# Weight conversion from 64-bit words: the sign set by a scaling of negative upper words on ScalarE instead of by a step of its own on VectorE

## The chip, the cores and the metric

The kernel runs on one core of a Trainium2 chip. The metric is the time of one execution on the device, in microseconds (us). The engines are named as the profile names them: PE is TensorE's matmul and PEld its weight load, DVE is VectorE, ACT is ScalarE, POOL is GpSimd, and SP is the queue that issues the DMAs. Each engine runs its own list of instructions strictly in order and waits on semaphores of the others.

## The reference, cut to what matters

The five weight matrices w_k, w_r, w_v, w_in and w_out come as float64, the other inputs as float32.

```python
scores = q @ k.T / sqrt(64); scores += minimum(-(cum_i - cum_j), 0), causal   # 4 x 8 heads, 576 rows
x = softmax(scores) @ v                                                       # 4 x 576 x 512
xk, xr = mix(x, x_prev, mu_k), mix(x, x_prev, mu_r)
y = sigmoid(xr @ w_r) * (relu(xk @ w_k) ** 2 @ w_v)
h = gelu(y @ w_in); u, v = halves of h
out = y + (u * (w_sg @ layernorm(v) * g + b)) @ w_out
```

## The kernel before, in words

The weights come to the chip as pairs of 32-bit words, and the kernel makes float32 values of them itself. A weight matrix is cut into parts of 128 rows by 512 columns: 8 of w_k (wk00 to wk31), 4 of w_r, 8 of w_v, 8 of w_in and 4 of w_out, 32 in all. `load_words` (L102) loads the words of one part, 512 KB, into a tile such as `wk00w`. `assemble` makes the float32 part in a buffer `cvt`: ACT scales the upper word, read as a float32 number, by 2^-112 (L111), which leaves room in the exponent; DVE shifts the bits left by 3 (L114), puts the sign bit of the upper word back (L115), and puts in the top 3 bits of the lower word (L116). `convert` then splits the part into a rounded half (ACT, L71 or L124) and the rest (DVE, L74 or L125), which the matmuls take.

The first 20 parts are converted while the first eight attention jobs run (a job is one pair of heads; the first four jobs are the first 320 rows of the first batch, the next four its other 256 rows, and from the ninth on a job has all rows of its batch). Two buffers `cvt` take turns. A load of words runs five parts ahead, and it is held back by a copy of one column (L101, DVE) from the `cvt` that was finished last into the tile that is to be loaded. The tiles of w_v lie where a table for the gate of the scores, `gt`, lay before; so the first of these copies, `wv00w`, also has to wait until the two DMAs that take that table away (`gate_d<-gt`, L320) have landed.

A job's scores go from PE (L362) through DVE (L377, mask and row minimum, in a bank of PSUM) to ACT (L404, exponential), PE (L442, transposes), ACT (L444, copies), PE (L446 and L450, products with v), DVE (L472, L473, L475) and back by PE and ACT (L478, L479) to the tile `xt`. When the first four jobs have their part of `xt`, the mixing (L617, L623, L71, L74) and the large matmuls (L685) can start. All engines work through lists that a scheduler of the builder has written out beforehand; a loop over priorities decides which work is near which. All DMAs are issued from SP's one list, each on one of eight semaphores in turn, and each waits for the transfer eight places ahead of it.

Of the kernel before, what the change touches and what calls it, by code (L numbers as in the profile page):

```python
# [8 lines left out]
F32 = mybir.dt.float32  # L9
# [4 lines left out]
AF = mybir.ActivationFunctionType  # L14
ALU = mybir.AluOpType
# [37 lines left out]
def block_kernel(ctx: ExitStack, tc: tile.TileContext, qkv, vb, s, w_r, w_k, w_v, mu, w_in, w_out, w_sgT, g_ln, b_sg, out):  # L53
# [6 lines left out]
    nc = tc.nc  # L60
# [44 lines left out]
    def assemble(w, c, n, t):  # L105

        pool, name, raw = w.parts[c][n]
        words = raw.bitcast(I32).rearrange("p (n t) -> p n t", t=2)
        hw, lw = words[:, :, 1], words[:, :, 0]
        ti = t.bitcast(I32)  # L110
        i = nc.scalar.mul(t, hw.bitcast(F32), 2.0**-112)  # L111
        if 0 < len(exps) <= GC:
            behind(i, exps[-1])
        nc.vector.tensor_scalar(ti, ti, 3, None, ALU.logical_shift_left)  # L114
        nc.vector.scalar_tensor_tensor(ti, hw, -0x80000000, ti, ALU.bitwise_and, ALU.bitwise_or)  # L115
        nc.vector.scalar_tensor_tensor(ti, lw, 29, ti, ALU.logical_shift_right, ALU.bitwise_or)  # L116
        return pool, name

    def convert(w, c, n, t):

        pool, name = assemble(w, c, n, t)
        half = pool.tile([P, 2, 512], F32R, tag=name, name=name)
        if w is wv:
            nc.scalar.mul(half[:, 0], t, 0.5)  # L124
            nc.vector.scalar_tensor_tensor(half[:, 1], t, 0.5, half[:, 0].bitcast(F32), ALU.mult, ALU.subtract)  # L125
        else:
            copy("A" if att is not None else "D", half[:, 0], t)
            minus(ENG["cl"], half[:, 1], t, half[:, 0])
        w.parts[c][n] = half
# [31 lines left out]
    def behind(i, j):  # L161

        kind = mybir.DependencyInfo(mybir.DependencyClass.NoSync, mybir.DependencyReason.DATA)
        tc.add_manual_dep(i.ins, j.ins.name, kind)
# [909 lines left out]
    def quarters(last):  # L1074

        ta = w1p.tile([P, 2, 512], F32, tag="wk01", name="cvt")
        tb = w1p.tile([P, 2, 512], F32, tag="wr30", name="cvt")
        for c in range(4):
            load_words(wo, c, 0)
        for c in range(4):  # L1080
            assemble(wo, c, 0, (ta, tb)[c // 2][:, c % 2])
        a11, a21, a12, a22 = (t[:, :, i * 256 : (i + 1) * 256] for t in (ta, tb) for i in range(2))

        def split(name, pool, tag, x):
            w = wq[name] = pool.tile([P, 2, 2, 256], F32R, tag=tag, name="w" + name)
            behind(nc.scalar.copy(w[:, 0], x), last[5 if name[0] == "s" else 3])
            minus("D", w[:, 1], x, w[:, 0])

        def fold(dst, x, y, op):
            nc.vector.tensor_tensor(dst, x, y, op)  # L1090

        split("11", w1p, "wk00", a11)
        split("12", w1p, "wk10", a12)
        split("22", w1p, "wk20", a22)
        fold(a22, a21, a22, ALU.add)
        split("s1", w1p, "wk30", a22)
        fold(a21, a11, a21, ALU.subtract)
        fold(a11, a22, a11, ALU.subtract)
        split("s3", xtp, "xh", a21)
        fold(a12, a12, a11, ALU.subtract)  # L1100
        split("s4", xtp, "xl", a12)
        split("s2", w1p, "wr30", a11)
# [93 lines left out]
```

## Time and profile before

| what | us |
| --- | --- |
| three timed runs | 679.87, 681.18 (median), 681.36 |
| the profiled execution, its time | 680.43 |
| its span, first to last instruction | 678.6 |
| busy: PE, DVE, ACT, POOL | 658.1, 543.2, 427.9, 48.3 |

The span is 1.8 us shorter than the profiled execution's own time, which lies 0.75 us below the median of the timed runs. PE is busy for 97% of the span, but the profile takes a waiting time inside a row of matmuls as busy, so the shares have to be read stage by stage.

### The profile page before, as it was taken

The page shows a single profiled execution, that of the slowest core. Times are in us where ns is not written, and L with a number is a line of the kernel's source. Part 1 is how long each engine was busy: PE and PEld are TensorE (multiplying, and loading weights), DVE is VectorE, ACT ScalarE, POOL GpSimd, SP SyncE. Part 2 cuts the span into 40 slices and gives each one's busy share as a digit, 9 for nine tenths or more (in the row PEclk, how much of TensorE's full clock was granted, in tenths as well). Part 3 has the DMA queues.
Part 4 walks back from the last instruction along what each step waited for, and adds up shares of the span by engine and source line. Part 5 has one row for each costly group of instructions (what it writes and reads, how often), then busy time and mean ns, then how long its engine had stood idle before and what let it go on. Part 6 is the DMA issues. An engine that isn't in the chain of part 4 may idle for free.

```text
span 678.6 us, 12902 instructions
## 1 busy us (share of the span) xinstructions
PE 658.1 (97%) x4590; PEld 613.2 (90%) x4590; DVE 543.2 (80%) x1396; ACT 427.9 (63%) x1014; POOL 48.3 (7%) x95
## 2 busy tenths in 40 slices
PE   7899999999999999999999999999999999999997
PEld 4667979798888989998999999999998998998997
DVE  8999988988889998898886696731788786958857
ACT  5788887779869987996895655714554423234222
POOL 6110000001110111011100000000000000000003
PEclk8899999999999999999999999999999999999999
DMA  8897132353343334333200840004131150340302
GB/s 269 265 300 233 40 105 73 106 156 98 106 132 94 110 96 115 119 95 101 86 24 19 297 134 35 1 18 159 54 122 36 44 167 1 112 135 0 97 1 71
DMA packets 41400, 71.66 MB, mean 106 GB/s; under 512 B 8244, under 2 KB 23968, under 8 KB 41304
## 3 DMA queue, kind: packets, MB, share of 16 engines
q1 hardware_dynamic: 41336, 70.84, 33.5%
q8 instruction: 36, 0.59, 0.4%
q14 instruction: 28, 0.23, 0.1%
HBM read 56.29 MB, written 10.19 MB: 98 GB/s over the span
## 4 chain that ended last, share of the span: by engine, by line
PE 73%; DVE 11%; DMA 5%; ACT 5%; issue 3%; SPq 1%; POOL 1%; POOLq 0%; DVEq 0%; ACTq 0%
PE m L685 28%; PE pu L698 8%; PE ps L995 3%; PE av L534 3%; PE t L549 3%; PE pg L959 3%; PE pg L960 2%; PE pg L958 2%; PE pv L890 2%; PE pv L889 2%; PE pv L888 2%; PE p L995 2%; PE av L450 2%; DVE ptl L553 2%; PE s L362 2%
## 5 line engine op out<-in xcount | busy, mean ns | idle before, releaser
L404 ACT ACTIVATE pr<-pr,nm 128x448 f32<-128x448 f32 (+4 forms) x144 | 84.8, 591 | 13.6 <-DVE nm L377 13.1
L685 PE MATMUL m<-xh,wk 128*128 128x288 f32 x512 | 87.4, 302 | 0.4 <-ACT kf L645 0.3
L685 PE MATMUL m<-kh,wv 128*128 128x288 f32 x512 | 79.3, 296 | 0.0
L685 PEld LDWEIGHTS m<-xh,wk 128*128 128x128 f32 x512 | 73.5, 189 | 2.8 <-ACT kf L645 1.0
L685 PEld LDWEIGHTS m<-kh,wv 128*128 128x128 f32 x512 | 71.9, 188 | 0.8
L377 DVE CUSTOM_DVE_ANT_0 pr<-s,mask 128x320 f32<-128x320 f32 (+3 forms) x128 | 60.4, 476 | 8.4 <-PE s L365 6.1
L74 DVE TENSOR_TENSOR xl<-xf,xh 128x288 fp32r<-128x288 f32 (+1 forms) x80 | 40.4, 519 | 18.5 <-ACT xh L824 12.7
L552 ACT CAST pth<-t 128x512 fp32r<-128x512 f32 (+1 forms) x72 | 38.0, 532 | 13.0 <-PE t L549 12.0
L645 ACT ACTIVATE kf<-m 128x288 f32<-128x288 f32 x64 | 26.1, 408 | 31.6 <-PE m L685 31.2
L685 PE MATMUL m<-xl,wk 128*128 128x288 f32 x256 | 45.9, 298 | 0.0
L553 DVE TENSOR_TENSOR ptl<-t,pth 128x512 fp32r<-128x512 f32 (+1 forms) x72 | 43.9, 615 | 2.4 <-ACT pth L552 2.0
L74 DVE TENSOR_TENSOR kl<-kf,kh 128x576 fp32r<-128x576 f32 x32 | 24.8, 775 | 23.8 <-ACT kh L71 23.7
L685 PE MATMUL m<-kl,wv 128*128 128x288 f32 x256 | 43.2, 298 | 0.0
L364 PE MATMUL s<-qk 128*128 128x288 f32 (+4 forms) x132 | 41.1, 313 | 1.0 <-DVE nh L377 0.4
L549 PE MATMUL t<-early,pr 128*128 128x128 f32 x252 | 39.0, 274 | 2.7 <-DVE ptl L553 2.6
L685 PE MATMUL m<-xh,wr 128*128 128x288 f32 x256 | 41.0, 299 | 0.4 <-ACT kf L645 0.3
L365 PE MATMUL s<-qk 68*128 68x288 f32 (+4 forms) x132 | 39.9, 308 | 0.4 <-DMA qk<-gate_d 0.4
L698 PE MATMUL pu<-xh,wi 128*128 128x288 f32 x256 | 40.2, 295 | 0.0
L617 ACT ACTIVATE xf<-xt,mu 128x288 f32<-128x288 f32 x64 | 33.6, 536 | 8.2 <-DVE xl L74 4.6
L685 PEld LDWEIGHTS m<-xl,wk 128*128 128x128 f32 x256 | 37.9, 188 | 0.7 <-issue 0.4
L959 PE MATMUL pg<-wg,vh 128*128 128x288 f32 x128 | 37.8, 295 | 0.0
L960 PE MATMUL pg<-wg,vl 128*128 128x288 f32 x128 | 37.7, 295 | 0.0
(330 smaller groups left out, 1757.3 us busy)
## 6 DMA issues: line engine op xcount, KB each, us to landing
qld<-qkv SPq DMA_DIRECT2D x24, 288.0 KB
kld<-qkv SPq DMA_DIRECT2D x24, 288.0 KB
x_d<-rt SPq DMA_DIRECT2D x8, 576.0 KB
xf<-x_d SPq DMA_DIRECT2D x8, 576.0 KB
vld<-qkv SPq DMA_DIRECT2D x24, 160.0 KB
qk<-qk SPq DMA_DIRECT2D x24, 144.0 KB
ot<-x_d SPq DMA_DIRECT2D x24, 144.0 KB
outT<-ot SPq DMA_DIRECT2D x24, 144.0 KB
```

Of the source, the lines that this page charges most:

```text
L74: (nc.gpsimd if pick(engines) == "P" else nc.vector).tensor_tensor(dst, a, b.bitcast(F32), ALU.subtract)
L364: nc.tensor.matmul(dst, qk[0][:, 0, qs], qk[0][:, 1, ks], start=True, stop=False)
L365: issued[0] = nc.tensor.matmul(dst, qk[1][0 : D + 4, 0, qs], qk[1][0 : D + 4, 1, ks], start=False, stop=True)
L377: nc.vector.tensor_tensor_reduce(out=dst, in0=src, in1=msk, scale=-0.125, scalar=first, op0=ALU.add, op1=ALU.min, accum_out=acc)
L404: i = nc.scalar.activation(dst, dst, AF.Exp, bias=nm[:, col : col + 1], scale=-1.0, accum_out=acc)
L549: issued[0] = nc.tensor.transpose(bank[:, o : o + P], x, ident)
L552: nc.scalar.copy(pth[:, cols], bank[:, 0:o])
L553: nc.vector.tensor_tensor(ptl[:, cols], bank[:, 0:o], pth[:, cols].bitcast(F32), ALU.subtract)
L685: i = nc.tensor.matmul(dst, w(x, c, m), xx[:, c], start=(n + c == 0), stop=(n == 2 and c == w.nk - 1))
L698: nc.tensor.matmul(dst, w(x, c, m), xx[:, c], start=(n + c == 0), stop=(n == 2 and c == w.nk - 1))
L959: nc.tensor.matmul(pg[:, 0:HD], vh[k][:, ds], wg[1][k][:, hs], start=False, stop=False)
L960: nc.tensor.matmul(pg[:, 0:HD], vl[k][:, ds], wg[0][k][:, hs], start=False, stop=False)
```

## The change

ACT's scaling becomes a Prelu with the same scale: positive values are only scaled, negative ones are multiplied by a further -2^32. Their result is positive and has one more bit set in its exponent field, and the shift left by 3 moves this bit into the place of the sign. The instruction that put the sign in is dropped.

```diff
         ti = t.bitcast(I32)
-        i = nc.scalar.mul(t, hw.bitcast(F32), 2.0**-112)
+        i = nc.scalar.activation(t, hw.bitcast(F32), AF.Prelu, scale=2.0**-112, alpha=-(2.0**32))
         if 0 < len(exps) <= GC:
             behind(i, exps[-1])
         nc.vector.tensor_scalar(ti, ti, 3, None, ALU.logical_shift_left)
-        nc.vector.scalar_tensor_tensor(ti, hw, -0x80000000, ti, ALU.bitwise_and, ALU.bitwise_or)
         nc.vector.scalar_tensor_tensor(ti, lw, 29, ti, ALU.logical_shift_right, ALU.bitwise_or)
         return pool, name
```

From the dropped line on, the lines of the changed kernel have a number that is one lower: its L115 is the former L116, L376 the former L377, L319 the former L320, and so on.

The scheduler writes the lists anew, and they differ in two stretches: from the first conversion to the start of the second batch's attention, and around the parts of w_in and w_out. Between these two stretches DVE's and ACT's lists are the same, instruction for instruction.

SP's list before, from the load of part wk31 to the load of `vb` for the fourth job. `gate_d<-gt` are the two DMAs for which the column copy `wv00w` waits, `kld`, `vld` and `qld` are inputs of the second batch:

```order
L102 DMA wk31w<-w_k 128x512
L213 DMA kld<-qkv 128x576
L223 DMA vld<-qkv 128x320
L102 DMA wr00w<-w_r 128x512
L213 DMA qld<-qkv 128x576
L213 DMA kld<-qkv 128x576
L223 DMA vld<-qkv 128x320
L320 DMA gate_d<-gt 16x4608 x2
L219 DMA vb<-vb 128x390
```

The same place in the list of the changed kernel:

```order
L102 DMA wk31w<-w_k 128x512
L102 DMA wr00w<-w_r 128x512
L212 DMA kld<-qkv 128x576
L222 DMA vld<-qkv 128x320
L212 DMA qld<-qkv 128x576
L212 DMA kld<-qkv 128x576
L222 DMA vld<-qkv 128x320
L319 DMA gate_d<-gt 16x4608
L102 DMA wr20w<-w_r 128x512
L319 DMA gate_d<-gt 16x4608
L218 DMA vb<-vb 128x390
```

The load of wr00w has moved ahead of four inputs, and that of wr20w, which stood eight places behind the second `gate_d`, now stands ahead of it. The second `gate_d` has the place eight behind the load of wr00w, where before it had the place eight behind wk31w.

DVE's list before, around the column copy `wv00w`. `pr` and `nm` are the scores of a job and their row minimum:

```order
L377 ISA pr_88,nm<-s,mask 128x192
L377 ISA nm 128x1
L114 TENSOR_SCALAR cvt<-cvt 128x512
L377 ISA pr_434,nm<-s,early 128x128
L377 ISA nm 128x1
L116 SCALAR_TENSOR_TENSOR cvt<-wk21w,cvt 128x512
L115 SCALAR_TENSOR_TENSOR cvt<-wk11w,cvt 128x512
L101 COPY wv00w<-cvt 128x1
L472 TENSOR_SCALAR rc<-av 128x4
L116 SCALAR_TENSOR_TENSOR cvt<-wk11w,cvt 128x512
```

The same place in the list of the changed kernel:

```order
L114 TENSOR_SCALAR cvt<-cvt 128x512
L115 SCALAR_TENSOR_TENSOR cvt<-wk11w,cvt 128x512
L376 ISA pr_89,nm<-s,mask 128x320
L376 ISA nm 128x1
L376 ISA pr_88,nm<-s,mask 128x192
L376 ISA nm 128x1
L101 COPY wr30w<-cvt 128x1
L101 COPY wv00w<-cvt 128x1
L74 TENSOR_TENSOR wk_405<-cvt,wk_405 128x512
L471 TENSOR_SCALAR rc<-av 128x4
```

The copy has kept its place against the scores of the third job, apart from the 128x128 block, which now comes after it; the conversion of wk11 is finished ahead of the copy instead of behind it.

SP's list before, a little later: from the load of wr20w to the inputs of the fifth job (`qk_86<-qkv`, `vb`):

```order
L102 DMA wr20w<-w_r 128x512
L102 DMA wr10w<-w_r 128x512
L204 DMA qk_86<-qkv 64x2x576
L207 DMA qk_86<-cur_d 1x576
L208 DMA qk_86<-cur_d 1x576
L102 DMA wv00w<-w_v 128x512
L204 DMA qk_86<-qkv 64x2x576
L219 DMA vb<-vb 128x650
```

The same place in the list of the changed kernel:

```order
L102 DMA wr10w<-w_r 128x512
L102 DMA wr30w<-w_r 128x512
L102 DMA wv00w<-w_v 128x512
L218 DMA vb<-vb 128x650
L203 DMA qk_86<-qkv 64x2x576
L206 DMA qk_86<-cur_d 1x576
L207 DMA qk_86<-cur_d 1x576
L203 DMA qk_86<-qkv 64x2x576
```

The fifth job's first input now stands behind three loads of words and its `vb`; before, it stood behind two loads of words.

## Rows read from the trace of the kernel before

**Rows 1.** The page's first two parts: busy time, and slices of 17 us.

```profile
PE 658.1 (97%) x4590; PEld 613.2 (90%) x4590; DVE 543.2 (80%) x1396; ACT 427.9 (63%) x1014; POOL 48.3 (7%) x95
DVE  8999988988889998898886696731788786958857
DMA  8897132353343334333200840004131150340302
```

**Rows 2.** Windows: stretch, its length, busy us (instructions) by engine, clock, DMA share, GB/s.

```profile
10.00:34.00 24.00, 20.64 (x109) 14.29 (x108) 21.63 (x68) 19.01 (x43) 3.69 (x7) 0.87 0.91 291
34.00:60.00 26.00, 24.49 (x148) 17.41 (x146) 25.42 (x84) 22.69 (x52) 2.23 (x3) 1.00 0.94 281
60.00:100.00 40.00, 38.74 (x274) 34.66 (x274) 37.15 (x97) 35.43 (x73) 0.00 (x0) 1.00 0.29 90
100.00:360.00 260.00, 253.11 (x1838) 239.36 (x1837) 228.83 (x607) 215.87 (x556) 25.75 (x42) 1.00 0.34 101
360.00:400.00 40.00, 39.70 (x294) 38.75 (x293) 27.54 (x58) 22.86 (x49) 1.60 (x2) 1.00 0.52 175
400.00:640.00 240.00, 240.00 (x1658) 231.02 (x1657) 169.66 (x416) 99.43 (x213) 0.00 (x0) 1.00 0.22 70
```

**Rows 3.** Windows of line L115 alone: DVE busy us (instructions).

```profile
0.00:34.00 34.00, 4.79 (x7) 0.90 0.85 267
34.00:100.00 66.00, 8.91 (x13) 1.00 0.54 165
370.00:400.00 30.00, 4.17 (x6) 1.00 0.66 223
400.00:490.00 90.00, 4.07 (x6) 1.00 0.17 57
```

**Rows 4.** Timeline of DVE: start, us, what, idle time before it.

```profile
31.61 0.28 DVE L377 CUSTOM_DVE_ANT_0 pr<-s,early 128x128 f32<-128x128 f32 x1
31.82 0.08 DVE L377 DVE_READ_ACCUMULATOR2_ANT nm<- 128x1 f32 x1
...
32.42 0.68 DVE L115 SCALAR_TENSOR_TENSOR cvt<-wk11w,cvt 128x512 int32<-128x512 int32 x1
34.04 0.15 DVE L101 COPY wv00w<-cvt 128x1 f32<-128x1 f32 x1 [0.94 <-DMA vb<-vb]
34.14 0.16 DVE L472 TENSOR_SCALAR rc<-av 128x4 f32<-128x4 f32 x1
34.22 0.68 DVE L116 SCALAR_TENSOR_TENSOR cvt<-wk11w,cvt 128x512 int32<-128x512 int32 x1
34.82 0.69 DVE L74 TENSOR_TENSOR wk<-cvt,wk 128x512 fp32r<-128x512 f32 x1
...
52.86 0.42 DVE L475 TENSOR_TENSOR avt<-av,rc 128x256 f32<-128x256 f32 x1
53.71 0.43 DVE L114 TENSOR_SCALAR cvt<-cvt 128x512 int32<-128x512 int32 x1 [0.43 <-ACT cvt L111]
54.05 0.68 DVE L115 SCALAR_TENSOR_TENSOR cvt<-wv00w,cvt 128x512 int32<-128x512 int32 x1
54.66 0.62 DVE L377 CUSTOM_DVE_ANT_0 pr<-s,mask 128x448 f32<-128x448 f32 x1
55.20 0.08 DVE L377 DVE_READ_ACCUMULATOR2_ANT nm<- 128x1 f32 x1
```

**Rows 5.** Timeline of SP's queue: when it issues which DMA.

```profile
20.65 0.38 SPq L102 DMA_DIRECT2D wk31w<-w_k  x1
...
24.21 1.88 SPq L320 DMA_DIRECT2D gate_d<-gt  x2
26.55 0.35 SPq L219 DMA_DIRECT2D vb<-vb  x1
```

**Rows 6.** The chain that ended last up to 110 us: by line, and one piece.

```profile
by line: PE m L685 14.6%; PE av L450 13.2%; PE s L362 11.5%; DMA vb<-vb 6.8%; DMA qld<-qkv 5.9%; PE t L442 3.8%; PE av L446 3.2%; DVE cvt L115 3.0%; issue 2.9%; DVE cvt L116 2.4%; DVE pr L377 2.3%; SPq L204 2.3%; DMA qk<-gate_d 2.0%; DVE wk
...
26.55 7.50 DMA vb<-vb
```

**Rows 7.** ACT by line: a table load, an exponential group, a scaling.

```profile
L264 ACT ACT_TABLE_LOAD  x1: 1283/1283/1283, 0.7 to 0.7; - x1
L404 ACT ACTIVATE pr<-pr,nm 128x576 f32<-128x576 f32 x8 | 6.2, 779 | 1.0 <-DVE nm L377 0.8
L111 ACT ACTIVATE cvt<-wk00w x1: 652/652/652, 11.5 to 11.5; 128x512 f32<-128x512 f32 x1
```

## What I predict, and why

> **What bounds the kernel now.** I read the page first. PE is busy for 97% of the span, and DVE's slices are fullest in the left half [rows 1]: the kernel has stages, and each has its own bound. The windows by stage say which. From 400 to 640 us PE is busy for all 240.00 us, so nothing that DVE or ACT gains there counts. From 100 to 360 us PE lacks 6.89 us, spread over attention work that the change doesn't touch. From 10 to 60 us it lacks 3.36 + 1.51 = 4.87 us, from 60 to 100 us 1.26 us, from 360 to 400 us 0.30 us [rows 2]. That is all that a faster conversion can find on PE: 4.87 + 1.26 + 0.30 = 6.4 us, plus what is hidden in matmuls that the profile lengthens while they wait.
>
> In the stretch from 10 to 60 us three things are nearly full: DVE with 21.63 of 24 and 25.42 of 26 us, the DMA engines with shares of 0.91 and 0.94, and ACT with 19.01 and 22.69 us [rows 2]. The page alone suggests DVE. But the one long idle time of DVE in it, 0.94 us, ends at 34.04 with a transfer [rows 4], and the chain of work holds a transfer of 7.50 us that ends at the same moment [rows 6]. So I ask of every microsecond that DVE saves whether a transfer lets it through.
>
> **What is removed.** L115 goes 32 times: 7 before 34 us, 13 from there to 100 us, 6 around w_in, 6 after 400 us [rows 3]. One lasts 0.68 us and holds the next instruction back by 0.60 (34.22 to 34.82 for its like, 54.05 to 54.66 for itself) [rows 4]. That frees 7 x 0.60 = 4.2 us of DVE before 34 us and 13 x 0.60 = 7.8 us up to 100 us. The 6 after 400 us lie under a PE that never waits: nothing. Those around w_in can give at most the 0.30 us that PE lacks there; I take 0.2.
>
> **What ACT pays.** The trace has no Prelu. Below, it costs what the scaling costs, 0.652 us; above, it costs what an ACT instruction with a per-row operand costs, 0.779 us for 576 columns [rows 7], scaled by 512/576 to 0.69 us, some 0.04 more, 0.8 us for 20 parts. It reads the same words and has constant operands like the scaling, so I take nothing.
>
> **What the first 4.2 us become.** DVE must pass the column copy wv00w, which waits for the two gate_d transfers. They were issued from 24.21 us on and let DVE go at 34.04 [rows 4, 5]. The name beside the wait, vb, is a transfer of SP's next row that DVE doesn't read; the table's own transfers stand directly ahead of it. DVE would reach the copy up to 3.8 us earlier than before (7 instructions less, 4.2 us; the end of wk11's conversion ahead of it, 0.6 us more; a 128x128 block behind it, 0.2 less). But the transfers don't come earlier: the loads ahead of them keep the DMA engines at a share of 0.91. They come later, for a load of 512 KB has moved ahead of the second one. At the 291 GB/s of this stretch [rows 2] its 524,288 bytes take 1.80 us; the lower bound is nothing, if it fills the 9% that is free; I take the part that is not, 1.80 x 0.91 = 1.6 us. DVE goes on at about 35.6 us, 1.6 us late, and all of the 4.2 us has turned into waiting. By the Trainium skill, "DMA: Bandwidth & Descriptors", Specifications, HBM gives a core some 358 GB/s; by that the load would take 1.46 us, and this stretch doesn't reach that rate.
>
> **From there to the large matmuls.** These wait for the fourth job's average, L475 at 52.86 us [rows 4]. Between the copy and this instruction DVE's list before held 4 L115, 5 L116 and 5 L114; the new list holds 7 low-word steps, 7 L114 and, besides, one rest of w_v, one block of scores of 448 and one of 128 columns. At the spacings of the timeline (0.60; 0.34 from 53.71; 0.54 from 54.66; 0.21 from 31.61) [rows 4] that is -2.4 + 1.2 + 0.7 + 0.6 + 0.5 + 0.2 = +0.8 us: the scheduler has filled what was freed with the next parts' conversion, ahead of attention. From L475 to the end of the mixing it is the other way. Two L115, a block of 448 columns and a rest of w_r are fewer, two rests of w_v and a shift more, and DVE's wait of 0.43 us for ACT at 53.71 falls away, if nothing new comes: -1.2 - 0.5 - 0.6 + 1.2 + 0.3 - 0.4 = -1.2 us. Sum at the start of the large matmuls: 1.6 + 0.8 - 1.2 = +1.2 us, later than before, with the conversions two or three parts ahead.
>
> **From 60 to 100 us** PE bounds, and it gets back most of the 1.26 us that it lacks, since DVE (37.15 of 40 us) has at least 7 L115 less, 4.2 us, and both have two or three parts less to do: -1.1 us. After 100 us the lists are the same; a shift is kept.
>
> **The sum.** +1.2 - 1.1 - 0.2 = -0.1 us, against the profiled execution's 680.43: 680.3 us. That execution was 0.75 us below the median of 681.18, so in the terms of the median 681.0 us. A change of 0.2%, 1.36 us, is about what a measurement here can tell from none; my forecast is no change.
>
> **Rivals.** *DVE is the bound and the saving comes through.* For it: DVE is busy for 25.42 of 26 us, and L115 itself holds 3.0% of the chain's first 110 us, 3.3 us [rows 2, 6]. Against it: the copy that waits for a transfer. It gives from -3.3 us to the 6.4 us that PE lacks in all: 674.8 to 677.9, in the middle 676.3. Chance 0.20. *A part of it:* the second gate_d isn't later than before, the term of 1.6 falls away, which gives -1.7 us, and from there to the -3.3 of the chain: in the middle -2.4, about 678.8. Chance 0.13.
>
> *Slower, by loads ahead of attention's inputs.* In the new list of SP the loads of wr10, wr30 and wv00 and its vb stand ahead of the first input of the fifth job; before, it had wr20 and wr10 ahead of it. At a DMA share of 0.94 from 34 to 60 us [rows 2] a load more is 524,288 bytes at 281 GB/s, 1.87 us. It decides as soon as the fifth job's scores wait for their input; PE then stands, and with it all that follows. With the 1.2 us above and half of what 60 to 100 us give back, it is +1.9 + 1.2 - 0.6 = +2.5 us: 683.7. Against it: attention is itself over a microsecond late there. Chance 0.24. *Slower by table loads:* if Prelu were not in the set that the exponential uses, ACT would change sets twice for each part among the exponentials, up to 40 x 1.283 us [rows 7] = 51 us before 100 us, and some 730 us in all. By the Trainium skill, "ScalarE: Activation LUTs", What ACT_TABLE_LOAD costs, every switch to a different set is such a load. The lists of both kernels hold two table loads each, at the same two places, so 0.03.
>
> *No change, as forecast:* 0.40, from 679.8 to 682.5.
>
> **Numbers.** The prediction is 681.0 us. The range goes from 675.8, inside the first rival, to 684.0, just past the slower one. Faster by over 0.2%: 0.20 + 0.13 = 0.33; slower: 0.24 + 0.03 = 0.27; within: 0.40.
>
> **What would show it.** Right: in the new timeline DVE reaches the copy wv00w near 30 us, stands for several microseconds, and goes on at 35 to 36 us; L475 of the fourth job is at 54 to 56 us; the last low-word step of w_v comes some microseconds earlier than before; PE's windows from 100 us on are as before; ACT's rows of L111 stay within 0.65 to 0.70 us. Wrong: DVE passes the copy before 33.5 us, or the stretch up to 100 us shows PE lacking under 4 us; or the scores of the fifth job wait for a DMA; or ACT shows more than two table loads.

## The result, and the profile after

The changed kernel takes 684.91 us (median of 6 runs, 682.97 to 687.36) against 680.31 us of the kernel before (6 runs, the three listed above among them): a ratio of 1.0066, 95% interval 1.0052 to 1.0081. It is 0.66% slower, some 4.5 us. The forecast was 681.0 us, no change, with 684.0 us as the upper end of the range. The profiled execution took 684.86 us, with a span of 683.1 us.

The page after, its first lines that answer [rows 1]:

```profile
PE 660.7 (97%) x4590; PEld 614.1 (90%) x4590; DVE 525.3 (77%) x1364; ACT 426.7 (62%) x1014; POOL 48.6 (7%) x95
...
DVE  8799676988899998889886594641578786957857
...
DMA  8898123352433333423200740004141150340302
```

DVE has 32 instructions and 17.9 us less to do, as the change promises, and the kernel is slower. The windows by stage, columns as in [rows 2]:

```profile
10.00:34.00 24.00, 20.95 (x108) 14.74 (x107) 18.84 (x64) 18.48 (x43) 3.67 (x6) 0.86 0.94 315
34.00:60.00 26.00, 22.64 (x128) 15.34 (x126) 24.05 (x80) 22.72 (x53) 2.34 (x4) 1.00 0.97 253
60.00:100.00 40.00, 39.32 (x277) 34.94 (x275) 29.44 (x81) 32.79 (x68) 0.00 (x0) 1.00 0.31 84
100.00:360.00 260.00, 252.25 (x1821) 237.41 (x1820) 226.16 (x600) 214.85 (x550) 24.75 (x40) 1.00 0.35 102
360.00:400.00 40.00, 39.75 (x285) 38.10 (x284) 27.16 (x61) 25.54 (x57) 2.81 (x5) 1.00 0.48 159
400.00:640.00 240.00, 240.00 (x1667) 231.52 (x1666) 162.69 (x402) 98.19 (x212) 0.00 (x0) 1.00 0.23 72
```

The loss begins from 34 to 60 us: PE lacks 3.36 us there, before 1.51 [rows 2], and does 128 matmuls instead of 148. The granted clock is no part of it: it is 1.00 in this stretch in both kernels, and 0.86 (before 0.87) in the stretch ahead of it. DVE is busy for 24.05 of 26 us although its sign steps are gone: the freed time was filled with later parts' conversions. From 60 to 100 us DVE falls from 37.15 to 29.44 us, which PE cannot use.

Windows of the large matmuls alone, PE and PEld busy with counts, and the start of the first and of the seventh of them; first after (L684), then before (L685):

```profile
60.00:100.00 40.00, 16.78 (x102) 14.18 (x102) 1.00 0.31 84
```

```profile
49.34 0.51 PE L684 MATMUL m<-xh,wk 128*128 128x288 f32 x2
60.97 0.90 PE L684 MATMUL m<-xh,wk 128*128 128x288 f32 x5
```

```profile
60.00:100.00 40.00, 18.58 (x106) 15.11 (x106) 1.00 0.29 90
```

```profile
46.65 0.51 PE L685 MATMUL m<-xh,wk 128*128 128x288 f32 x2
60.40 0.64 PE L685 MATMUL m<-xh,wk 128*128 128x288 f32 x3
```

The first of them starts at 49.34 us, before at 46.65: 2.7 us late. The seventh, which was the first behind the fourth job's average (52.86) before, is 0.6 us late. DVE's timeline after; L474 is the average of a job (the former L475), here of the third and the fourth, and further down of the seventh and eighth:

```profile
31.04 0.15 DVE L101 COPY wr30w<-cvt 128x1 f32<-128x1 f32 x1
33.76 0.15 DVE L101 COPY wv00w<-cvt 128x1 f32<-128x1 f32 x1 [2.58 <-DMA vb<-vb]
...
46.69 0.46 DVE L376 CUSTOM_DVE_ANT_0 pr<-s,mask 128x288 f32<-128x288 f32 x1 [1.34 <-PE s L361]
...
47.91 0.42 DVE L474 TENSOR_TENSOR avt<-av,rc 128x256 f32<-128x256 f32 x1
...
55.11 0.42 DVE L474 TENSOR_TENSOR avt<-av,rc 128x256 f32<-128x256 f32 x1
...
98.64 0.42 DVE L474 TENSOR_TENSOR avt<-av,rc 128x256 f32<-128x256 f32 x1
110.30 0.42 DVE L474 TENSOR_TENSOR avt<-av,rc 128x256 f32<-128x256 f32 x1
```

Before, the third, seventh and eighth of them stood here:

```profile
44.37 0.42 DVE L475 TENSOR_TENSOR avt<-av,rc 128x256 f32<-128x256 f32 x1
...
95.64 0.42 DVE L475 TENSOR_TENSOR avt<-av,rc 128x256 f32<-128x256 f32 x1
105.73 0.42 DVE L475 TENSOR_TENSOR avt<-av,rc 128x256 f32<-128x256 f32 x1
```

The column copy is 0.28 us earlier than before, after 2.58 us of waiting instead of 0.94 [rows 4]; 14 us later the third job's average is 3.5 us late, the fourth's 2.25, the seventh's 3.0, the eighth's 4.6. (The sixth's, at 86.58 instead of 85.68, is only 0.9 late.) DVE's row at 46.69 shows one reason: in DVE's list the fifth job's scores stand ahead of the third job's average, and they wait. SP's queue and the chain of work of the changed kernel tell for what; a row of PE is put between them:

```profile
23.61 0.44 SPq L319 DMA_DIRECT2D gate_d<-gt  x1
24.84 0.33 SPq L102 DMA_DIRECT2D wr20w<-w_r  x1
26.19 0.33 SPq L319 DMA_DIRECT2D gate_d<-gt  x1
...
33.61 0.36 SPq L102 DMA_DIRECT2D wr10w<-w_r  x1
34.44 0.36 SPq L102 DMA_DIRECT2D wr30w<-w_r  x1
...
35.41 0.38 SPq L218 DMA_DIRECT2D vb<-vb  x1
35.88 0.60 SPq L203 DMA_DIRECT2D qk<-qkv  x1
...
45.90 0.62 SPq L203 DMA_DIRECT2D qk<-qkv  x1
```

```profile
45.93 1.21 PE L361 MATMUL s<-qk 128*128 128x288 f32 x4 [0.97 <-DVE rc L471]
```

```profile
27.76 5.97 DMA vb<-vb
...
35.41 8.35 DMA vb<-vb
43.78 7.71 DMA wv20w<-w_v
51.51 5.77 DMA wv40w<-w_v
```

Each DMA waits for the transfer eight places ahead of it. Eight places behind the fifth job's first input (35.88) stands the one at 45.90; it could only go when that input had landed, and PE's scores of the fifth job start at 45.93. So the input took 10 us. The chain from 27 to 57 us is nearly all transfers; before, it held one there, of 7.50 us [rows 6].

The same rule tells what the column copy waited for, beside which the profile names vb. The load eight places behind the second gate_d went at 33.61, the one eight places behind vb at 34.44; DVE went on at 33.76, when the table had gone and vb had not landed. Before, the two loads went at 33.81 and 34.34, and DVE at 34.04 [rows 4]:

```profile
33.81 0.36 SPq L102 DMA_DIRECT2D wr20w<-w_r  x1
34.34 0.36 SPq L102 DMA_DIRECT2D wr10w<-w_r  x1
```

ACT's groups of the changed kernel: the two table loads, and the slowest and a usual Prelu; below them the slowest scaling of the kernel before:

```profile
L263 ACT ACT_TABLE_LOAD x1 | 1.3, 1283 | 0.7 <-PEq L1188 0.7
L891 ACT ACT_TABLE_LOAD x1 | 1.3, 1283 | 0.0
L111 ACT ACTIVATE cvt<-wv30w 128x512 f32<-128x512 f32 x1 | 0.7, 698 | 0.0
...
L111 ACT ACTIVATE cvt<-wv10w 128x512 f32<-128x512 f32 x1 | 0.7, 675 | 0.0
```

```profile
L111 ACT ACTIVATE cvt<-wv60w 128x512 f32<-128x512 f32 x1 | 0.7, 703 | 0.0
```

The 32 Prelus take 0.649 to 0.698 us, the 32 scalings before took 0.652 to 0.703: the same. There are two table loads, as before.

### The profile page after: what moved, and what is told of

It reads as the page before. It is cut to its first block, busy times and chain, and to the rows that moved or that the text cites. A ratio compares the mean times of both kernels' runs of the same rounds, so it can differ in the third digit from the quotient of the medians.

```text
span 683.1 us, 12877 instructions
## 1 busy us (share of the span) xinstructions
PE 660.7 (97%) x4590; PEld 614.1 (90%) x4590; DVE 525.3 (77%) x1364; ACT 426.7 (62%) x1014; POOL 48.6 (7%) x95
## 4 chain that ended last, share of the span: by engine, by line
PE 70%; DVE 11%; DMA 7%; ACT 6%; issue 3%; POOL 1%; SPq 1%; POOLq 0%; DVEq 0%; ACTq 0%
PE m L684 27%; PE pu L697 7%; PE ps L994 3%; PE av L533 3%; PE pg L958 2%; PE pg L959 2%; PE pg L957 2%; PE pv L887 2%; PE pv L889 2%; PE pv L888 2%; PE t L548 2%; PE p L994 2%; DMA vb<-vb 2%; DVE qk L74 2%; DVE ptl L552 2%
## 5 line engine op out<-in xcount | busy, mean ns | idle before, releaser
L684 PE MATMUL m<-xh,wk 128*128 128x288 f32 x512 | 85.9, 300 | 0.0
L684 PE MATMUL m<-kh,wv 128*128 128x288 f32 x512 | 79.4, 297 | 0.0
L684 PEld LDWEIGHTS m<-xh,wk 128*128 128x128 f32 x512 | 73.2, 189 | 1.3 <-issue 0.4
L684 PEld LDWEIGHTS m<-kh,wv 128*128 128x128 f32 x512 | 71.7, 188 | 0.8
L376 DVE CUSTOM_DVE_ANT_0 pr<-s,mask 128x320 f32<-128x320 f32 (+3 forms) x128 | 60.4, 475 | 12.8 <-PE s L364 4.8
L684 PE MATMUL m<-xl,wk 128*128 128x288 f32 x256 | 46.2, 299 | 0.0
L684 PE MATMUL m<-kl,wv 128*128 128x288 f32 x256 | 43.1, 298 | 0.0
L684 PE MATMUL m<-xh,wr 128*128 128x288 f32 x256 | 41.2, 300 | 0.5 <-ACT kf L644 0.5
L684 PEld LDWEIGHTS m<-xl,wk 128*128 128x128 f32 x256 | 38.0, 188 | 0.9 <-issue 0.6
```

The costliest lines, as they stand in the source:

```text
L376: nc.vector.tensor_tensor_reduce(out=dst, in0=src, in1=msk, scale=-0.125, scalar=first, op0=ALU.add, op1=ALU.min, accum_out=acc)
L684: i = nc.tensor.matmul(dst, w(x, c, m), xx[:, c], start=(n + c == 0), stop=(n == 2 and c == w.nk - 1))
```

## The experiments

The scheduler rewrites four lists at once, so the runs take its lists apart. In the changed kernel an ordering edge, without any wait of its own, is drawn from each instruction to the one that shall stand ahead of it:

```diff
     project(*tail)
+    kind = mybir.DependencyInfo(mybir.DependencyClass.NoSync, mybir.DependencyReason.DATA)
+    named = {i.name: i for i in nc.cur_bb.bb.instructions}
+    for row in ORDER.split("/")[:-1]:
+        row = [f"I-{n}" for n in row.split() if f"I-{n}" in named]
+        for i, j in zip(row[1:], row):
+            tc.add_manual_dep(named[i], j, kind)
```

ORDER holds, for each engine, the numbers of its instructions in the wanted order, up to the second batch's attention. "Lists of before" are those of the kernel before without the sign steps; the lists around w_in and w_out stay those of the changed kernel. All ratios are to runs of the kernel before on the same chip, with 95% intervals; the kernel before had medians of 680.56 to 680.94 us there, and 680.31 beside the changed kernel. A point is one per cent of its time, 6.8 us; differences between runs on different chips are taken in points.

| run | lists of PE, DVE, ACT | SP's list | us | ratio |
| --- | --- | --- | --- | --- |
| e1, sign step kept | before | before | 681.81 | 1.0011 (1.0000 to 1.0023) |
| e2 | before | before | 681.41 | 1.0012 (1.0001 to 1.0023) |
| e3 | before | after | 682.34 | 1.0027 (1.0013 to 1.0042) |
| e4 | after | before | 687.37 | 1.0094 (1.0076 to 1.0113) |
| changed kernel | after | after | 684.91 | 1.0066 (1.0052 to 1.0081) |

### The instruction alone: e1 and e2

```diff
-        i = nc.scalar.mul(t, hw.bitcast(F32), 2.0**-112)
+        i = nc.scalar.activation(t, hw.bitcast(F32), AF.Prelu, scale=2.0**-112, alpha=-(2.0**32))
```

> The kernel before with ACT's scaling replaced by the Prelu, and DVE's sign step kept (it sets a bit that is already set). All lists stand as in the kernel before. Theory Q (SP's new list brings attention's inputs late): 680.3 us, no change. Theory E (the new order on PE, DVE and ACT puts conversions ahead of attention's steps): 680.3 us, no change. Theory P (the Prelu itself, or the words it writes, costs time): 683 to 685 us.

> The changed kernel (Prelu, no sign step), with the lists of PE, DVE, ACT and SP held in the order of the kernel before up to the second batch's attention. Theories Q and E: the loss is gone; DVE has 20 steps of 0.60 us less, of which at most the 3.3 us that they held of the chain come through: 677 to 680.3 us. Theory P: 683 to 685 us.

The Prelu with the sign step kept takes 681.81 us, without it, in the same order, 681.41 us: no difference that can be measured. Both are 0.1% above before, with intervals that begin at 1.0000 and 1.0001, so up to 0.2% may be left for the Prelu; the changed kernel loses 0.66%. So neither the Prelu nor the missing step makes the loss, and 20 steps less on DVE bring nothing; I had expected 677 to 680.3 us of e2. e1 is written without the edges and e2 with them, so they cost nothing that shows either. DVE's row and a piece of the chain of e2 show where they go:

```profile
33.22 0.15 DVE L101 COPY wv00w<-cvt 128x1 f32<-128x1 f32 x1 [2.46 <-DMA vb<-vb]
```

```profile
43.39 10.26 DMA qk<-qkv
```

DVE stands 2.46 us at the column copy for the gate's table, and the sixth job's input, issued at 43.39 us, lets PE go 10.26 us later. Up to there a part of the saving had come through: the fourth average stands at 52.04 us, 0.8 us earlier than before.

### SP's list or the engines' lists: e3 and e4

> The changed kernel with PE, DVE and ACT held in the order of the kernel before up to the second batch's attention, but SP's list as the scheduler of the changed kernel writes it (loads of words ahead of the inputs of the fifth to seventh jobs). Theory Q: nearly the whole loss is there, 682.5 to 685 us, and PE waits for the fifth job's input. Theory E: the loss is gone, 677 to 681 us.

> The changed kernel with PE, DVE and ACT in its own order, but SP's list held in the order of the kernel before up to the second batch's attention. Theory Q: the loss is gone, 678 to 681 us. Theory E: nearly the whole loss is there, 682.5 to 685 us.

SP's list alone costs 0.15 points, 1.0 us (e3 less e2); e3 lies between its two ranges. The engines' lists alone cost 0.82 points, 5.6 us (e4 less e2), more than either theory had; with the SP list that was written along with them it is less, 684.91 us. My theory Q, that the loads ahead of attention's inputs make the loss, is true for the smaller part. In e3 PE stands once for 2.56 us, and the clock falls behind it:

```profile
32.00:36.00 4.00, 2.45 (x13) 1.34 (x12) 0.99 (x4) 0.24 (x2) 0.00 (x0) 1.00 0.59 173
36.00:40.00 4.00, 2.99 (x8) 1.91 (x9) 3.70 (x13) 2.85 (x6) 0.79 (x1) 0.61 0.84 258
```

### Conversions or attention: e5, e6, e13, e16

e5 keeps the changed kernel's order, but draws an edge from each L111 to the step of attention at whose place in ACT's list it stood before. e6 holds PE's list and the order of all steps but the conversions as before, and leaves the conversions free; SP's list is that of the changed kernel in both.

> The changed kernel with its own lists of PE and SP and its own order of attention's and mixing's steps on DVE and ACT; only the conversions are held back: ACT's scaling of each part may not stand ahead of the place among attention's steps that it had in the kernel before. Theory E1 (the conversions' early places on ACT and DVE push attention back): the loss goes, 681 to 683 us. Theory E2 (the order of PE's list, with scores of the fourth and fifth jobs ahead of the third job's products): the loss stays, 684 to 686 us.

> The other way round: the changed kernel with its own list of SP, but with PE's list and the order of attention's and mixing's steps on DVE and ACT as in the kernel before; only the conversions stand where the scheduler likes, as early as in the changed kernel or earlier. Theory E1: the loss stays, 684 to 687 us. Theory E2: the loss goes, 681 to 683 us.

e5 took 690.54 us (1.0147), e6 687.21 us (1.0100). Both edits were slower than the changed kernel, e5 far above both of its ranges and e6 at the end of theory E1's. e6 and e3 differ in the conversions' places alone: early conversions cost 0.73 points there, 5.0 us. One row of ACT in e6, with the row behind it, shows one way:

```profile
58.03 0.67 ACT L111 ACTIVATE cvt<-wv40w 128x512 f32<-128x512 f32 x1 [1.31 <-DMA wv40w<-w_v]
58.61 0.76 ACT L403 ACTIVATE pr<-pr,nm 128x576 f32<-128x576 f32 x1
```

A scaling stands early in the list, its words have not landed, and an exponential of attention behind it waits along. But e5 does not allow the turn that late conversions mend the order of the changed kernel: theory E1 in this simple form falls.

e13 mends the third job's place by hand: scores of the fourth and fifth jobs behind its products, two scalings behind its copies, its average ahead of the fifth job's scores.

> The changed kernel with all its own lists, but for one place: on PE the scores of the fourth and fifth jobs stand behind the products and the back transposes of the third job, on ACT two scalings (wr20, wr10) stand behind the third job's second copy of its probabilities instead of between the two, and on DVE the third job's average (L471, L472, L474) stands ahead of the fifth job's scores. If the third job's lateness carries the loss: 681.5 to 683 us, and the large matmuls start 2 to 3 us earlier than in the changed kernel. If the loss arises again behind it (conversions of w_v waiting for words): 684 to 685.5 us.

It took 687.67 us (1.0110), because the mending made a wait of its own (PE's waits from 24 to 75 us; columns: us in total, times, longest):

```profile
PE t L465 <- ACT xt L466: 2.7, 1, 2.7
```

So it says nothing on the third job's place. e16 leaves all to the scheduler but for one edge on each scaling:

```diff
+ORDER = (
+    "234 239 "
+    "/ "
+    "248 254 "
+    "/ "
...
```

These are the first two of 20 pairs: a step of attention, and the L111 that must stay behind it.

> The changed kernel, written anew by its scheduler with one more rule: ACT's scaling of each of the first 20 parts stays behind the step of attention that it follows in the kernel before. Everything else is free. If the conversions' early places alone cause the loss: 680.5 to 682 us. If the scheduler's new order of attention's steps loses by itself: 683.5 to 688 us.

686.74 us (1.0075, 1.0056 to 1.0094): with the scalings late the scheduler writes attention in a third order, unlike that of before and that of the changed kernel, and it is as slow as the changed kernel. The conversions' places alone are not the cause.

### The transfers: e7 to e12, e14, e15, e17

Five inputs of the second batch, 1184 KB, are issued from 21 to 24 us, between the first two rows of [rows 5] and so ahead of the gate's table. The first that is read is vld, in the kernel before at 82.8 us:

```profile
L71 ACT CAST vv<-vld x4: 444/458/460, 82.8 to 124.1; 128x320 fp32r<-128x320 f32 x4
```

These runs issue the five behind the last load of w_v. In rows of SP's list:

```diff
 L102 DMA wk31w<-w_k 128x512
-L212 DMA kld<-qkv 128x576
-L222 DMA vld<-qkv 128x320
 L102 DMA wr00w<-w_r 128x512
-L212 DMA qld<-qkv 128x576
-L212 DMA kld<-qkv 128x576
-L222 DMA vld<-qkv 128x320
 L319 DMA gate_d<-gt 16x4608 x2
...
 L102 DMA wv70w<-w_v 128x512
+L212 DMA kld<-qkv 128x576
+L222 DMA vld<-qkv 128x320
+L212 DMA qld<-qkv 128x576
+L212 DMA kld<-qkv 128x576
+L222 DMA vld<-qkv 128x320
```

> The changed kernel with all lists as in the kernel before (as in the run with the lists of before), except that five inputs of the second batch, 1184 KB that SP issued at 21 to 24 us and that nobody reads before 82 us, are issued behind the last load of w_v. Theory D (up to 60 us the transfers bound, and what DVE saves turns into waiting for them): transfers come up to 4.2 us earlier (1184 KB at 291 GB/s) and the saving of DVE comes through: 676.5 to 679.5 us. Without D: 680.5 to 682 us, as with the lists of before.

> The kernel before (scaling and sign step) in its own order, with the same five inputs of the second batch issued behind the last load of w_v. Theory D: DVE becomes the bound of the stretch instead of the transfers; part of the time comes, 678.5 to 680.5 us, and it stays 1 to 3 us above the run without the sign step: that is then what the sign step is worth. Without D: 680.7 us, no change.

e7 took 678.56 us (0.9973, 0.9960 to 0.9985), e8, with the sign step, 679.04 us (0.9984, 0.9975 to 0.9993). In e7 DVE passes the copy without a wait, 2.4 us earlier than in e2, and PE lacks 1.03 us from 34 to 60 us instead of 2.80 in e2 (the copy and the window of e7, then the window of e2):

```profile
30.78 0.15 DVE L101 COPY wv00w<-cvt 128x1 f32<-128x1 f32 x1
```

```profile
34.00:60.00 26.00, 24.97 (x153) 18.23 (x154) 22.45 (x74) 23.04 (x54) 1.44 (x3) 1.00 0.91 258
```

```profile
34.00:60.00 26.00, 23.20 (x138) 16.17 (x139) 22.67 (x77) 22.10 (x51) 1.62 (x3) 1.00 0.94 242
```

So the transfers did bound. The sign step is still worth only 0.1 points (0.9984 less 0.9973), 0.5 us by the medians, with intervals that overlap; I had expected 1 to 3.

e9 to e11 take the column copy of wv00w away:

```diff
-        if after is not None:
+        if after is not None and name != "wv00":
```

> The changed kernel with the lists of before, without the one column copy of wv00w on DVE: its load waits on SP's own list for the gate's table to go, at the same place; DVE no longer stands there (2.5 us in the run with the lists of before). If that wait is what swallows DVE's saving: 678.5 to 680.5 us. If the work behind it waits for other transfers anyway: 680.7 to 682 us.

> Both together: the changed kernel with the lists of before, the five inputs of the second batch deferred, and without the column copy of wv00w. If DVE's standing at the copy still counts once the transfers are relieved: 676 to 678 us. If not: 678 to 679.2 us, as with the deferred inputs alone.

> The same two edits on the kernel before, with scaling and sign step. It tells what the sign step is worth once nothing on DVE waits for the gate's table and the transfers are relieved: if DVE is then the bound, 1 to 3 us more than the run without the sign step (677.5 to 680 us); if PE and ACT bound anyway, less than 1 us more.

e9 took 681.52 us (1.0012), the same as e2: the 2.46 us of waiting were not what swallowed the saving. DVE waits elsewhere instead, 2.3 us at once for PE's transposes:

```profile
DVE pr L376 <- PE t L441: 2.9, 2, 2.3
```

e10 took 678.88 us (0.9966, 0.9953 to 0.9978), e11, with the sign step, 679.26 us (0.9975, 0.9964 to 0.9986). Again 0.1 points for the sign step, with intervals that overlap. All four runs beat both kernels: e7 and e10 are 0.3% faster than the kernel before, e8 and e11 0.2%.

> The changed kernel with all its own lists, except that the five inputs of the second batch, which it too issues ahead of the gate's table, go behind its last load of w_v. If its order only loses because transfers land later than its scheduler supposed: 677 to 680 us, as with the order of before. If its order loses by itself: 681.5 to 684 us, as much above the deferred run in the order of before as now.

> The same mending, with the five inputs of the second batch deferred as well (without the mending this gave 681.9 us). If the third job's place carries what is left of the loss: 678.5 to 680 us. If not: 681 to 682.5 us.

> PE's list and the order of attention's steps as in the kernel before, the five inputs deferred, and only the conversions where the scheduler likes, as early as in the changed kernel or earlier (with them at their places of before this gave 678.6 us). If early conversions lose only because their words are not there: 678 to 680 us. If they lose because they stand ahead of attention's steps on ACT and DVE: 681.5 to 684 us.

> The same rule, with the five inputs of the second batch issued behind the last load of w_v. If the conversions' early places alone cause the loss: 678 to 679.5 us. If the order of attention's steps loses by itself: 681 to 685 us.

The changed kernel with the inputs deferred, e12, took 681.94 us (1.0015, 1.0003 to 1.0027): it gains 0.51 points, the kernel before (e8) 0.16. Of the 0.66 points by which the changed kernel is slower, 0.31 are left when both have the transfers relieved (1.0015 less 0.9984). e17, the scalings held, gains still more, 0.57 points, to 682.16 us (1.0018). e14 took 685.76 us (1.0077), above both ranges; it carries e13's own wait. e15, which differs from e7 in the conversions' places alone, took 686.50 us (1.0085, 1.0067 to 1.0102): 1.1 points, 7.6 us, for early conversions with relieved transfers, more than I had expected. In its profiled execution the clock was lower in this stretch:

```profile
34.00:60.00 26.00, 24.17 (x124) 16.91 (x122) 21.71 (x71) 19.79 (x45) 2.67 (x4) 0.87 0.79 228
```

PE did 124 matmuls in this stretch, e7 153. The clock is at most a small part of it: over the whole span e15's five runs had granted clocks from 0.989 to 0.997, and all of them took 686.06 to 686.87 us.

### Any other order: e18

```diff
-C0, RATE, LEAD, AHEAD = 0.7, 1.1, 0.0, 5
+C0, RATE, LEAD, AHEAD = 0.6, 1.1, 0.0, 5
```

> The kernel before, instruction for instruction, with its sign step; only the constant C0, which says how many conversions the list asks for at each step of attention, is 0.6 instead of 0.7, so that the scheduler writes another order from the first conversion on. If any order but that of before loses in this stretch: 683 to 689 us. If the loss belongs to the conversions that the changed kernel pulls forward: 680 to 682 us.

It took 681.71 us (1.0016, 1.0007 to 1.0026): the kernel before in another order of its scheduler loses a quarter of what the changed kernel loses. That the old order was merely left is no sufficient cause.

## Why the prediction was wrong

**The Prelu and the table loads.** Right: 0.649 to 0.698 us for one, and no load added; e1 is within 0.2%. By the Trainium skill, "ScalarE: Activation LUTs", What ACT_TABLE_LOAD costs, a load is paid for every switch to a different set; the trace agrees as far as it goes: two loads in both kernels, so the Prelu brought no switch.

**The first 4.2 us turn into waiting.** Right in kind: DVE reaches the copy at 31.1 us and stands for 2.58 us. The term of +1.6 us was wrong: DVE goes on at 33.76, 0.28 us earlier than before instead of 1.6 later. The load of wr20w went ahead of the second gate_d, but the stretch moved 315 GB/s instead of 291 [rows 2], and SP issued the first gate_d at 23.61 us instead of 24.21 [rows 5]. And e9 shows that this wait, on which I had hung the argument, decides nothing: without it the time is the same.

**From the copy to the large matmuls.** This is the step that failed. I added up DVE's instructions between the copy and the fourth average (+0.8) and behind it (-1.2), as if DVE alone set the end of each step. The fourth average came at 55.11, 2.25 us late; 2.4 had been summed, but that the two agree is luck: the terms are -0.3 for the copy and +2.5 for what lies behind it, three times what I had there. The scheduler had rewritten PE's and ACT's lists too, and the sum took nothing from them: the fifth job's scores stand ahead of the third job's average and wait for their input until 45.93. Nor is the fourth average what all large matmuls wait for: six of them start ahead of it, the first at 46.65 before. These are late by 2.7 to 3.8 us, and the sum has no term for them; the seventh is late by 0.6 instead of the 1.2 summed, but PE comes to it with some 20 matmuls fewer done (236 from 10 to 60 us instead of 257 [rows 2]). In place of DVE's instruction count the runs show: DVE's missing steps 0 (e1, e2), SP's list 1.0 us (e3), and the engines' new lists 5.6 us by themselves (e4) and some 2.7 us beside SP's new list (0.66 points less e3's 0.27).

**60 to 100 us give back 1.1 us.** Wrong. PE's missing time did fall, from 1.26 to 0.68 us, but the lateness stayed: the seventh average is 3.0 us late, and PE has done 102 large matmuls in the stretch instead of 106. Of all matmuls it did 277 instead of 274, so that three of some 20 were won back. I had booked missing time of the kernel before as time to be won, while the changed kernel came to it late.

**After 100 us and w_in.** Nearly right: 0.9 us more missing from 100 to 360 us, and 0.05 us less from 360 to 400. Nearly all of the 0.9 lies from 100 to 110 us, where PE is busy for 9.18 us instead of 10.00.

**The rivals.** The one that I held against it, loads of words ahead of the fifth job's input, had the right sign and with 683.7 us nearly the right time; the fifth job's scores did wait for a DMA, which I had named as a sign against me. But e3 gives SP's list 1.0 us, so that the time was near by luck; its price also left out the 325 KB of vb that stand ahead as well, another 1.2 us at 281 GB/s. The rival that DVE's saving comes through (0.20) is refuted: in the same order 20 steps less bring nothing that can be measured, and with relieved transfers some 0.5 us. The one that a part of it does, since the second gate_d is not later (0.13; the middle of its two ends is -2.5 us, not -2.4), had its condition met, and still nothing came. The 3.0% that L115 held of the chain [rows 6] was no price: in e2 the steps are gone and the time is not.

**What stays open.** Shown: the loss lies in the new lists of the first 100 us and not in the instructions; about half of it (0.35 of 0.66 points) is there only as long as the transfers are late; early conversions cost 0.7 to 1.1 points when the other steps keep the order of before. Not shown: one place of PE's, DVE's or ACT's list that carries the other half. Moving conversions alone (e5, e16) or one job alone (e13) made it slower; that the four lists are matched to each other, so that none can be moved by itself, would explain this, but no run shows it. That the scheduler puts conversions early because it supposes transfers to land sooner than they do fits e6 and e12, but is argued only.

## What to carry to other kernels

When a scheduler writes the lists, an instruction removed is two changes, the instruction and the new order: hold the old order and time the first alone before believing a saving. Look at who fills the freed time and what stands behind that in an in-order list, on all engines, not only on the one that was relieved. And where transfers keep their engines at 0.9 and more, look first for bytes that nobody reads soon: deferring five inputs brought more than 32 instructions less.

## What was not expected of the hardware

The granted clock was 0.61 in a stretch of 4 us in which PE came out of 2.56 us of idle time (e3); in the kernel before and the changed one it was 1.00 from 34 to 60 us. The levels are 2.4 and 1.2 GHz, so 0.61 says that most of the stretch ran at the lower. Such a pause costs more than its own length: the two score matmuls of 320 columns behind it took 1.44 us, in the kernel before 0.81. In e15 two idle times of PE of 0.86 and 0.65 us, at 40.7 and 41.6 us, stood ahead of a stretch from 44 to 48 us with a clock of 0.50. An input of 288 KB needed 10 us from issue to landing while the DMA engines' share was 0.97.
